# Forward column products as pairs of 64-row matmuls, one load queue at the head, a longer warm-up and a new order

## The chip, the core and the metric

The kernel runs on one core of one Trainium2 chip. The metric is the time of one execution in device microseconds; a figure for a kernel is the median of its runs. The core has a matrix engine (TensorE, PE in the profile), three engines for elementwise work (VectorE or DVE, ScalarE or ACT, GpSimd or POOL) and SyncE (SP), which here issues nearly all DMA transfers, one after the other, in one queue. Each engine works through its own list of instructions in order and waits on semaphores for the others.

## The reference

```python
x = A_x                                   # 1 x 2048 x 640, bf16
xn = _layernorm(x, axis=-1)               # rows of 640
X = rfft2(xn.astype(float32), axes=(-2, -1)) * (A_w_r + 1j * A_w_i)    # 2048 x 321
y = irfft2(X, s=(2048, 640)).astype(bfloat16)
h = (xn @ B_w_gate) * (xn @ B_w_up)       # 640 -> 1536
return x + y + h @ B_w_down               # 1536 -> 640
```

Two branches share the normalized rows: a filter in the two-dimensional frequency domain, and a gated product of matrices.

## The kernel before

**Tiling.** The 2048 rows are 16 blocks of 128. Partition p of block j holds row 16 p + j, so that a load of several blocks reads long pieces of memory. All matrix operands are bf16; PSUM has eight banks of 512 float32 values per partition.

**The work, by its names.** Every piece of work is a task with a name. Loads have names in ld_: ld_x (rows), ld_gw (gate and up weights; the first number is the first of 12 groups of 128 columns, the second is 0 for gate and 1 for up), ld_w (filter), ld_wd (down weights), ld_tf, ld_ti, ld_fd, ld_g, ld_sm1 (constant tables), ld_xr (rows again, for the final sum).

- Head. A warm-up task (L711 to L718) runs 40 matmuls of 128 columns on constants while the first rows load. Rows are normalized: for some blocks VectorE takes statistics (bn, ag), for others ScalarE does (sm at L738, sq at L747); ScalarE takes the root (sd, L772), VectorE the reciprocal (rs, L780) and the scaled rows (mul, L797). Blocks 0 to 3 are transposed by PE (T0, L816) and copied out of PSUM (eT0); blocks 4 to 15 by DMA transposes (xt, L804). After T0_0 a filler of six matmuls of 64 columns (L705) runs.
- Gated product. GU_f_b_w multiplies column group f, gate (w = 0) or up (w = 1), with the transposed rows from block b on: for single blocks and pairs of blocks two column groups at a time (L974, 128 or 256 columns), else 512 columns (L952). eG copies them to SBUF, H (L992, L994) multiplies gate by up.
- Forward transform. S1 to S5 on VectorE (L858 to L893) are the butterflies over the 640 columns, for groups of two or four blocks: S_0 blocks 0 and 1, S_1 blocks 2 and 3, S_2, S_3 and S_4 four blocks each. R_b (L906) is the column product of block b: five matmuls, each with 128 x 128 values of S's result as the stationary operand and a 128 x 128 table as the moving one. eR (through the copy helper L681 or L682) takes the 640 results per partition, a bank and a quarter of the next, to the buffer U. When all 16 R are done, D (L1035), C (L1054) and WM (L1071, L1074, with the filter) follow in eight rounds.
- Backward transform. SM, J, IA (L1117), I (L1145), then V1 to V5 on VectorE.
- Closing stage. ACC (L1222) is the down product, in three pieces of a chain of 12, which wait for ld_wd; IV (L1234) adds the inverse transform into the same bank; FINA and FIN add x, and st_out writes.

The table of R is half zeros: a block holds 64 x 2 rows that alternate along the partitions, and the transform is over 64, so for each parity the entries of the other are zero:

```python
fw = np.zeros((_R, _RR, 16, _G, 2, _RR), np.float64)      # _R = 64, _RR = 2
fw[:, r, tt, g, 0, r] = np.cos(ang)
```

**What sets the order.** The order of all tasks on all engines, and the PSUM bank of each, is written out by hand in the list _PLAN (L405): triples of task, engine and bank. replay (L151) assigns them; compute_waits (L196) makes the semaphore waits that the data and banks need. So each engine, and SP's queue, runs a fixed sequence, and a late task holds back all that stands behind it on its engine.

Around the change the sequences are: SP issues ld_x0a, ld_x1, ld_x2, ld_gw0_0, ld_x3, ld_gw2, ld_x4, ld_gw4, ld_x5, ld_sm1, ld_gw6_1, ld_gw8_1, ld_gw6_0, then xt7 (which waits for mul7), and then ld_gw8_0. ScalarE's queue issues ld_x0b and ld_gw0_1. VectorE runs both halves of bn1 between ag0 and rs_0. PE runs T0_1 after the filler, then GU_0_0; both GU_2_2 before R_0, R_1. The runs of R on PE, with GU between them, are R_0 R_1, R_2 R_3, R_6 R_4 R_7, R_5, R_10 R_11 R_8, R_9, R_12 R_13 R_15, R_14.

Of the kernel before, what the change touches and what calls it, by code (L numbers as in the profile page):

```python
# [241 lines left out]
_R = 64  # L242
_S1 = _S // _R
_RR = _S1 // 16
_G = 64 // _S1
# [10 lines left out]
def _build_tables():  # L256
# [6 lines left out]
    fw = np.zeros((_R, _RR, 16, _G, 2, _RR), np.float64)  # L263
    bw = np.zeros((16, _G, 2, _RR, _R, _RR), np.float64)
    for tt in range(16):
        for g in range(_G):
            q = tt * _G + g
            ang = two_pi * ((q * s2) % _R) / _R
            for r in range(_RR):
                fw[:, r, tt, g, 0, r] = np.cos(ang)  # L270
                bw[tt, g, 0, r, :, r] = np.cos(ang)
                if q:
                    fw[:, r, tt, g, 1, r] = -np.sin(ang)
                    bw[tt, g, 1, r, :, r] = np.sin(ang)
                else:
                    fw[:, r, tt, g, 1, r] = np.cos(math.pi * s2)
                    bw[tt, g, 1, r, :, r] = np.cos(math.pi * s2)
    sm[:, 1, :] = fw.reshape(128, 128)
# [122 lines left out]
def _d_act(n):  # L401
# [4 lines left out]
    (11, 4, -1), (10, 0, 5), (18, 2, -1), (12, 1, -1), (19, 2, -1), (20, 2, -1), (8, 3, -1), (0, 3, -1), (13, 4, -1),  # L406
    (28, 2, -1), (27, 2, -1), (14, 4, -1), (169, 4, -1), (15, 4, -1), (170, 1, -1), (21, 1, -1), (36, 1, -1), (22, 2, -1),
    (29, 2, -1), (30, 1, -1), (171, 4, -1), (172, 4, -1), (23, 2, -1), (24, 0, 0), (9, 0, 2), (37, 1, -1), (25, 1, -1),
    (38, 1, -1), (31, 2, -1), (32, 2, -1), (33, 0, 3), (26, 2, -1), (179, 0, 5), (39, 2, -1), (34, 2, -1), (40, 2, -1),
    (35, 2, -1), (43, 1, -1), (44, 1, -1), (45, 1, -1), (46, 2, -1), (47, 2, -1), (181, 0, 1), (182, 1, -1), (180, 1, -1),  # L410
    (183, 2, -1), (112, 2, -1), (41, 0, 7), (42, 1, -1), (189, 0, 6), (191, 0, 2), (184, 0, 0), (192, 1, -1), (190, 1, -1),
    (193, 2, -1), (48, 0, 4), (16, 4, -1), (186, 0, 1), (51, 2, -1), (50, 2, -1), (49, 1, -1), (185, 1, -1), (187, 1, -1),
    (188, 2, -1), (52, 2, -1), (54, 2, -1), (113, 2, -1), (53, 2, -1), (62, 1, -1), (63, 1, -1), (194, 0, 7), (64, 1, -1),
    (196, 0, 6), (174, 4, -1), (173, 4, -1), (55, 2, -1), (197, 1, -1), (195, 1, -1), (198, 2, -1), (114, 2, -1), (65, 1, -1),
    (204, 0, 0), (206, 0, 5), (56, 1, -1), (115, 2, -1), (57, 2, -1), (58, 2, -1), (116, 2, -1), (201, 0, 3), (205, 1, -1),
    (202, 1, -1), (66, 1, -1), (207, 1, -1), (199, 0, 2), (200, 1, -1), (208, 2, -1), (203, 2, -1), (67, 2, -1), (70, 2, -1),
    (211, 0, 1), (212, 1, -1), (17, 4, -1), (1, 4, -1), (72, 1, -1), (209, 0, 4), (117, 0, 0), (210, 1, -1), (118, 1, -1),
    (73, 1, -1), (74, 1, -1), (119, 0, 2), (121, 2, -1), (176, 4, -1), (221, 0, 7), (178, 4, -1), (175, 4, -1), (213, 2, -1),
    (216, 0, 5), (120, 1, -1), (217, 1, -1), (122, 2, -1), (68, 2, -1), (123, 2, -1), (75, 1, -1), (214, 0, 1), (215, 1, -1),
    (218, 2, -1), (124, 2, -1), (82, 1, -1), (76, 1, -1), (77, 2, -1), (125, 2, -1), (78, 2, -1), (71, 4, -1), (177, 4, -1),  # L420
    (59, 4, -1), (219, 0, 6), (60, 2, -1), (80, 2, -1), (226, 0, 4), (222, 1, -1), (220, 1, -1), (223, 2, -1), (224, 0, 0),
    (227, 1, -1), (225, 1, -1), (228, 2, -1), (130, 2, -1), (229, 0, 1), (230, 1, -1), (126, 0, 6), (127, 1, -1), (83, 1, -1),
    (128, 0, 2), (129, 1, -1), (231, 0, 0), (232, 1, -1), (233, 2, -1), (131, 2, -1), (236, 0, 4), (467, 4, -1), (237, 1, -1),
    (84, 1, -1), (85, 1, -1), (92, 1, -1), (234, 0, 5), (235, 1, -1), (238, 2, -1), (469, 4, -1), (69, 4, -1), (432, 4, -1),
    (3, 4, -1), (61, 4, -1), (86, 1, -1), (436, 4, -1), (87, 2, -1), (132, 2, -1), (241, 0, 7), (242, 1, -1), (93, 1, -1),
    (94, 1, -1), (246, 0, 2), (4, 4, -1), (431, 4, -1), (81, 4, -1), (239, 0, 3), (440, 4, -1), (240, 1, -1), (243, 2, -1),
    (244, 0, 4), (245, 1, -1), (247, 1, -1), (249, 0, 5), (251, 0, 0), (95, 1, -1), (96, 1, -1), (252, 1, -1), (250, 1, -1),
    (254, 0, 3), (255, 1, -1), (256, 0, 2), (257, 1, -1), (133, 2, -1), (248, 2, -1), (261, 0, 7), (134, 2, -1), (139, 0, 5),
    (135, 0, 0), (141, 0, 3), (97, 2, -1), (88, 2, -1), (90, 2, -1), (253, 2, -1), (266, 0, 2), (140, 1, -1), (262, 1, -1),
    (468, 4, -1), (437, 4, -1), (438, 4, -1), (472, 4, -1), (470, 4, -1), (100, 2, -1), (98, 2, -1), (258, 2, -1), (143, 2, -1),  # L430
    (142, 1, -1), (137, 0, 6), (138, 1, -1), (259, 0, 5), (260, 1, -1), (263, 2, -1), (144, 2, -1), (102, 1, -1), (267, 1, -1),
    (136, 1, -1), (264, 0, 6), (265, 1, -1), (268, 2, -1), (145, 2, -1), (269, 0, 5), (103, 1, -1), (270, 1, -1), (276, 0, 7),
    (277, 1, -1), (104, 1, -1), (271, 0, 1), (272, 1, -1), (273, 2, -1), (146, 2, -1), (274, 0, 0), (105, 1, -1), (275, 1, -1),
    (106, 1, -1), (147, 2, -1), (107, 2, -1), (281, 0, 3), (282, 1, -1), (279, 0, 7), (280, 1, -1), (284, 0, 0), (285, 1, -1),
    (286, 0, 2), (152, 0, 0), (153, 1, -1), (278, 2, -1), (473, 4, -1), (108, 2, -1), (435, 4, -1), (434, 4, -1), (466, 4, -1),
    (442, 4, -1), (439, 4, -1), (2, 4, -1), (91, 4, -1), (99, 4, -1), (154, 0, 6), (155, 1, -1), (89, 4, -1), (441, 4, -1),
    (79, 4, -1), (101, 4, -1), (110, 2, -1), (283, 2, -1), (156, 2, -1), (148, 0, 3), (149, 1, -1), (287, 1, -1), (289, 0, 5),
    (288, 2, -1), (157, 2, -1), (294, 0, 0), (295, 1, -1), (150, 0, 6), (291, 0, 1), (292, 1, -1), (290, 1, -1), (293, 2, -1),
    (296, 0, 4), (151, 1, -1), (297, 1, -1), (298, 2, -1), (301, 0, 0), (299, 0, 2), (309, 0, 1), (471, 4, -1), (109, 4, -1),
    (111, 4, -1), (433, 4, -1), (302, 1, -1), (300, 1, -1), (158, 2, -1), (7, 4, -1), (310, 1, -1), (311, 0, 3), (304, 0, 4),  # L440
# [81 lines left out]
def _build(nc, A_x, A_w_r, A_w_i, B_w_gate, B_w_up, B_w_down, out, opts=None):  # L522
# [3 lines left out]
    with es:  # L526
# [128 lines left out]
        b_sd = sch.buf("sd", 10 ** 9 + 30, 1)  # L655
        b_ve = sch.buf("ve", 10 ** 9 + 40, 1)

        xv = A_x[0].rearrange("(p j) d -> p j d", j=16)
        ov = out[0].rearrange("(p j) d -> p j d", j=16)
        wvs = [w_.rearrange("(k1 k2) l -> k1 k2 l", k2=_R) for w_ in (A_w_r, A_w_i)]  # L660
        gvs = [w_.rearrange("(j p) f -> p j f", p=128) for w_ in (B_w_gate, B_w_up)]
# [684 lines left out]
```

## Time and profile before

| what | value |
|---|---|
| median of three runs | 199.5 us (198.73 to 199.68) |
| profiled execution | 199.59 us |
| its span, first to last instruction | 197.9 us |
| mean granted TensorE clock | 0.991 |
| busy: PE, DVE, ACT | 192.2, 175.4, 137.9 us |
| DMA | 23.73 MB, mean 120 GB/s |

Some starts and ends, by the trace, in us: warm-up 0.85 to 5.06; T0_0 5.63; T0_1 7.44; first GU 7.88; mul0 5.18 to 5.57; mul3 ends 10.64; S5_0 ends 21.07; R_0 21.21; mul9 ends 30.0; xt5, the last of blocks 4 to 7, lands 36.8; first GU of blocks 4 to 7 38.2; S5_4 ends 69.35; R_12 69.61; first D 72.9; last IA 134.5; last matmul 195.4.

A line of the groups gives the source line, the engine, the operation, its tiles and shapes, the number of instructions, then busy us and mean ns of one, then the idle time before them and what ended it. A line of the timeline begins with start and duration. A line of the chain is a piece of the sequence of waits that ended last. Matmuls overlap: one lasts 219 ns at 128 columns, while the next starts 56 ns after it, so durations of PE are not its rate; starts are.

### The profile page before, as it was taken

To read this page: it belongs to the slowest core of one execution; us is meant where nothing else is said; L and a number is where in the kernel's file an instruction comes from. 1 tells how busy PE (TensorE), PEld (TensorE's weight loads), DVE (VectorE), ACT (ScalarE), POOL (GpSimd) and SP (SyncE) were. 2 spreads that over 40 slices of the span, in tenths; PEclk is the share of its full clock that TensorE was granted. 3 is DMA by queue.
4 is the path that set the end of the run, shared out by engine and by line. 5 is a ranking of instruction groups with operands and counts; after the bars stand their busy time and mean duration, and the time that the engine had idled before them with its cause. 6 is when DMAs were issued, how large, how long until landed. Compare 5 with 4: busy or idle time off the path is not lost.

```text
span 197.9 us, 4118 instructions
## 1 busy us (share of the span) xinstructions
PE 192.2 (97%) x1587; PEld 123.4 (62%) x1587; DVE 175.4 (89%) x364; ACT 137.9 (70%) x280; POOL 13.1 (7%) x22
## 2 busy tenths in 40 slices
PE   8699989999999999999999999999999999999995
PEld 8598735454454465556555555558677777777764
DVE  3588999999999989999999999985999999999843
ACT  3879998998976479998899998967504541440340
POOL 1000000000000000320330320330000000000000
PEclk9889999999999999999999999999999999999999
DMA  6999364979412016238492524004101252034242
GB/s 176 332 372 319 50 167 105 190 156 123 96 33 70 3 46 180 68 94 259 127 247 60 151 65 136 0 0 137 65 3 61 74 165 79 34 122 134 71 162 66
DMA packets 29666, 23.73 MB, mean 120 GB/s; under 512 B 10448, under 2 KB 27600, under 8 KB 29520
## 3 DMA queue, kind: packets, MB, share of 16 engines
q1 hardware_dynamic: 28848, 23.08, 43.8%
q10 hardware_dynamic: 800, 0.41, 0.7%
q8 instruction: 12, 0.20, 0.4%
q14 instruction: 6, 0.05, 0.1%
HBM read 18.89 MB, written 2.62 MB: 109 GB/s over the span
## 4 chain that ended last, share of the span: by engine, by line
PE 84%; DMA 7%; DVE 4%; ACT 3%; SPq 1%; issue 0%
PE ps L952 44%; PE ps L1222 25%; PE ps L1117 3%; PE ps L1035 2%; DMA arena<-in_B_w_gate_dram 2%; DMA arena<-in_B_w_down_dram 2%; PE ps L1054 2%; PE ps L1234 2%; PE ps L974 2%; DMA arena<-in_A_x_dram 2%; PE ps L906 2%; PE ps L1145 1%; ACT arena L738 1%; ACT arena L681 1%; DVE arena L797 1%; PE ps L816 1%
## 5 line engine op out<-in xcount | busy, mean ns | idle before, releaser
L681 ACT ACTIVATE arena<-ps 128x512 bf16<-128x512 f32 (+6 forms) x217 | 113.3, 579 | 50.8 <-PE ps L1234 18.0
L952 PE MATMUL ps<-arena 128*128 128x512 bf16 x420 | 97.4, 379 | 0.6 <-DMA arena<-in_B_w_gate_dram 0.6
L952 PEld LDWEIGHTS ps<-arena 128*128 128x128 bf16 x420 | 38.9, 98 | 42.1 <-DMA arena<-in_B_w_gate_dram 1.1
L1222 PE MATMUL ps<-arena 128*128 128x320 bf16 (+2 forms) x396 | 57.1, 295 | 0.2 <-DMA arena<-in_B_w_down_dram 0.2
L1222 PEld LDWEIGHTS ps<-arena 128*128 128x128 bf16 x396 | 37.4, 98 | 13.8 <-issue 0.5
L1071 DVE TENSOR_TENSOR arena<-ps,arena 128x256 bf16<-128x256 f32 x64 | 22.6, 415 | 1.9 <-PE ps L1054 1.8
L992 DVE TENSOR_TENSOR arena<-arena 128x512 bf16<-128x512 bf16 x42 | 17.9, 433 | 1.2 <-ACT arena L681 0.5
L974 PE MATMUL ps<-arena 128*128 128x128 bf16 (+1 forms) x160 | 15.3, 262 | 0.0
L974 PEld LDWEIGHTS ps<-arena 128*128 128x128 bf16 x160 | 13.7, 107 | 1.2
L682 POOL COPY arena<-arena 64x252 bf16<-64x252 bf16 x8 | 4.5, 568 | 100.7 <-DVE arena L1088 100.6
L1261 DVE TENSOR_TENSOR arena<-arena 128x640 bf16<-128x640 bf16 x15 | 7.1, 488 | 4.1 <-ACT arena L681 4.0
L747 ACT ACTIVATE arena<-arena 128x640 bf16<-128x640 bf16 x12 | 10.0, 836 | 0.1
L738 ACT ACTIVATE arena<-arena 128x640 bf16<-128x640 bf16 x12 | 8.9, 744 | 1.2 <-DMA arena<-in_A_x_dram 1.1
L1117 PEld LDWEIGHTS ps<-arena 128*128 128x128 bf16 x160 | 7.8, 116 | 2.5 <-ACT arena L681 0.2
L682 DVE CAST arena<-ps 128x320 bf16<-128x320 f32 (+3 forms) x11 | 7.0, 662 | 2.3 <-PE ps L1117 1.4
L1101 POOL TENSOR_SCALAR arena<-arena 64x252 bf16<-64x252 bf16 x8 | 7.9, 991 | 17.8 <-DVE arena L1088 17.4
L1117 PE MATMUL ps<-arena 128*128 128x64 bf16 x160 | 8.3, 198 | 0.0
L1035 PEld LDWEIGHTS ps<-arena 128*128 128x128 bf16 x160 | 6.5, 98 | 2.6 <-issue 0.3
L858 DVE TENSOR_TENSOR arena<-arena 128x768 f32<-128x768 bf16 (+1 forms) x10 | 7.9, 792 | 0.0
L1234 PE MATMUL ps<-arena 128*128 128x320 bf16 (+2 forms) x33 | 7.8, 295 | 0.0
L1035 PE MATMUL ps<-arena 128*128 128x64 bf16 (+1 forms) x160 | 7.0, 193 | 0.0
L1074 DVE TENSOR_TENSOR arena<-ps,arena 128x260 bf16<-128x260 f32 x16 | 7.0, 435 | 0.0
(61 smaller groups left out, 184.5 us busy)
## 6 DMA issues: line engine op xcount, KB each, us to landing
arena<-in_A_x_dram SPq DMA_DIRECT2D x19, 160.0 KB, 2.9
arena<-in_A_w_r_dram SPq DMA_DIRECT2D x30, 80.2 KB, 2.5
arena<-in_A_w_i_dram SPq DMA_DIRECT2D x30, 80.2 KB, 2.5
out_dram<-arena SPq DMA_DIRECT2D x15, 160.0 KB, 2.3
arena<-in_B_w_gate_dram SPq DMA_DIRECT2D x4, 320.0 KB, 6.3
arena<-in_A_x_dram SPq DMA_DIRECT2D x1, 1280.0 KB, 10.1
arena<-c_tf SPq DMA_DIRECT2D x4, 256.0 KB, 3.8
arena<-c_ti SPq DMA_DIRECT2D x2, 512.0 KB, 5.0
```

Source lines behind the costliest of these rows:

```text
L681: return c.e.activation(dst, src, _ACTF.Copy)
L682: return c.e.tensor_copy(dst, src)
L738: return c.e.activation(v_jk, v_x[:, b, :], _ACTF.Copy, scale=1.0 / _D, accum_out=v_m32[:, b:b + 1])
L747: return c.e.activation(v_jk, v_x[:, b, :], _ACTF.Square, scale=-1.0, bias=v_m32[:, b:b + 1], accum_out=v_ss[:, b:b + 1])
L952: ins = c.e.matmul(ps[:, bk, :], v_gw[:, w, j, ft, :], v_xt[:, j, rows], start=(j == 0), stop=(j == 4))
L974: ins = c.e.matmul(ps[:, bk, i * n:(i + 1) * n], v_gw[:, w, j, ft0 + i, :], v_xt[:, j, rows], start=(j == 0), stop=(j == 4))
L992: return c.e.tensor_tensor(v_ht[:, ft0, rows], gb[:, 0, :], gb[:, 1, :], _OP.mult)
L1035: ins = c.e.matmul(ps[:, bk + i, k * 64:k * 64 + n], v_uq[:, k, t + i, :], v_fd[:, k * 128 + w * n: k * 128 + w * n + n], start=True, stop ...
L1071: c.e.tensor_tensor(dst, xh, wv, _OP.mult)
L1117: ins = c.e.matmul(ps[:, bk, 64 * k:64 * k + 64], yl, v_ti[:, q, 0, :], start=True, stop=True)
L1222: ins = c.e.matmul(ps[:, bk, 0:sl3.stop - sl3.start], v_ht[:, ft, a * 128:(a + 1) * 128], v_wd[:, ft, sl3], start=(ft == _FT_ORDER[0]), st ...
L1234: return c.e.matmul(ps[:, bank_of(own), 0:sl3.stop - sl3.start], v_sm[:, 2, :], v_v[:, a, sl3], start=False, stop=True)
```

## The change

- R uses 64 rows at a time. Partitions now hold the two parities apart: partition r * 64 + s of block j holds row 32 s + 16 r + j (loads of x, the second loads of x, and the stores of the result are permuted so). The table of R becomes 128 x 64 without the zeros. Each of the five matmuls becomes two, one on partitions 0 to 63 into a bank and one on 64 to 127 into the next, each with 64 columns. eR reads the two banks interleaved, element by element. The table of IV is permuted to match.
- All gate and up loads go through SP; before, ld_gw0_1 was issued by ScalarE.
- The warm-up has 45 matmuls instead of 40, the filler five instead of six, and T0_1 comes after the filler by a dependence.
- The durations with which the planner reckons and _PLAN are new. SP: ld_x0a, ld_x2, ld_x1, ld_x3, ld_gw0_0, ld_gw0_1, ld_gw2, ld_x4, ld_gw4_1, ld_sm1, ld_gw4_0, ld_x5, ld_gw6, ld_gw8_1, ld_gw8_0, xt7, ld_w0_1_0, xt5, two filter loads, xt4, xt6; later ld_ti1 stands ahead of xt10, and ld_wd4 behind ld_wd6, ld_xr1 and ld_xr2. VectorE: rs_0 and mul0 before bn1, and both copies of T0_0 and eG_0_0 are its own; mul4 after S5_0; H_44 to H_47 spread over V1 to V5. PE: GU_0_0_0 before T0_1, one GU_2_2 after R_1 and R_0. The runs of R are now R_1 R_0, R_2 R_3, R_6 R_4, R_7 R_5, R_9 R_8, R_11, R_10, R_15 R_12 R_13, R_14. A few copies change between ScalarE and VectorE.

```diff
-    fw = np.zeros((_R, _RR, 16, _G, 2, _RR), np.float64)
-    bw = np.zeros((16, _G, 2, _RR, _R, _RR), np.float64)
+    fw = np.zeros((_RR, _R, 16, _G, 2), np.float64)
+    bw = np.zeros((16, _G, 2, _RR, _RR, _R), np.float64)
...
-                fw[:, r, tt, g, 0, r] = np.cos(ang)
-                bw[tt, g, 0, r, :, r] = np.cos(ang)
+                fw[r, :, tt, g, 0] = np.cos(ang)
+                bw[tt, g, 0, r, r, :] = np.cos(ang)
...
-    sm[:, 1, :] = fw.reshape(128, 128)
+    sm[:, 1, 0:64] = fw.reshape(128, 64)
...
 _PLAN = (
-    (11, 4, -1), (10, 0, 5), (18, 2, -1), (12, 1, -1), (19, 2, -1), (20, 2, -1), (8, 3, -1), (0, 3, -1), (13, 4, -1),
...
+        v_un = V("U").rearrange("p (n a c r) -> p n a c r", a=16, c=2, r=2)
...
-        xv = A_x[0].rearrange("(p j) d -> p j d", j=16)
-        ov = out[0].rearrange("(p j) d -> p j d", j=16)
+        xv = A_x[0].rearrange("(s r j) d -> r s j d", r=2, j=16)
+        ov = out[0].rearrange("(s r j) d -> r s j d", r=2, j=16)
...
-        nwarm = opts.get("nwarm", 10)
+        nwarm = opts.get("nwarm", 45)
...
-            for i in range(4 * nwarm):
+            for i in range(nwarm):
...
-                if b == 0:
-                    for f in fills:
-                        f.deps.add(t0)
+                if b < len(fills):
+                    fills[b].deps.add(t0)
+                if 0 < b <= len(fills):
+                    t0.deps.add(fills[b - 1])
...
-                        ins = c.e.matmul(psflat[:, bk * 512 + k * 128: bk * 512 + (k + 1) * 128], st, v_sm[:, 1, :],
-                                         start=True, stop=True)
+                        for r in range(2):
+                            ins = c.e.matmul(ps[:, bk + r, 64 * k:64 * k + 64],
+                                             st[64 * r:64 * r + 64], v_sm[64 * r:64 * r + 64, 1, 0:64],
+                                             start=True, stop=True)
...
-                    src = psflat[:, bk * 512: bk * 512 + 640].rearrange("p (j q m) -> p j q m", j=5, q=_NQ)
-                    return copy_on(c, v_u[:, :, :, b, :], src)
+                    src = ps[:, bk:bk + 2, 0:320].rearrange("p r (n c) -> p n c r", c=2)
+                    return copy_on(c, v_un[:, :, b], src)
...
-                    q="act" if w_ and i < 1 else "sp")
+                    q="sp")
```

## The prediction

> **What bounds the kernel now.** I read the page first, then the chain by time, the timeline of the first 20 us, and the groups by form.
>
> ```profile
> span 197.9 us, 4118 instructions
> PE 192.2 (97%) x1587; PEld 123.4 (62%) x1587; DVE 175.4 (89%) x364; ACT 137.9 (70%) x280; POOL 13.1 (7%) x22
> ```
>
> TensorE (PE) carries the chain (84% of it by the page), but its busy time says little, because matmuls overlap; starts say more. By the timeline PE starts the first real product (L974) at 7.88 us and the last matmul at about 195.4. From 12 us on its stream has few holes: 0.73 us before 29.00 and 0.37 before 139.87, both counted between starts, and 0.15 or less elsewhere. VectorE (DVE) idles, by its timeline, only some 2 us between 10.6 and 69 us: it is a second bound, close behind.
>
> ```profile
> 5.69 0.74 ACT L738 ACTIVATE arena<-arena 128x640 bf16<-128x640 bf16 x1 [1.11 <-DMA arena<-in_A_x_dram]
> ...
> 6.73 0.17 DVE L780 RECIPROCAL arena<-arena 128x1 f32<-128x1 f32 x1 [1.16 <-ACT arena L773]
> ...
> 7.44 0.45 PE L816 MATMUL ps<-arena 128*128 128x128 bf16 x5 [1.17 <-DVE arena L797]
> ...
> 7.88 2.13 PE L974 MATMUL ps<-arena 128*128 128x128 bf16 x20
> ```
>
> This is the head in the timeline: block 2 of x lands at 5.66, ScalarE (ACT) waits for it, VectorE waits for ACT, and PE for both. The 20 products at 7.88 take 2.13 us, 107 ns each, where later ones take 56. The stages tell why:
>
> ```profile
> 5.00:8.00 3.00, 1.26 (x20) 0.95 (x20) 1.46 (x8) 2.31 (x8) 0.00 (x0) 1.00 1.14 311
> 8.00:11.40 3.40, 3.40 (x35) 3.40 (x34) 2.24 (x8) 3.15 (x8) 0.00 (x0) 0.51 1.10 349
> 11.40:20.00 8.60, 8.60 (x108) 8.04 (x107) 7.42 (x23) 7.54 (x21) 0.00 (x0) 0.99 1.07 343
> ```
>
> (Length, then PE, weight loads, VectorE, ACT, GpSimd busy, clock, DMA.) After a stretch with PE busy 1.26 of 3.00 us, the granted clock is half for 3.4 us: 1.7 us of work lost.
>
> ```profile
> 23.91 0.29 SPq L804
> ...
> 24.26 4.70 DMA arena<-in_B_w_gate_dram
> ...
> 29.00 1.25 PE ps L952 x5
> ```
>
> In the chain, the last gate load stands on SP behind the transpose xt7, which waits for VectorE: hence PE's 0.73 us hole. Further on in the same chain ten matmuls of L906 (the column products R) take 0.56 us, 56 ns each.
>
> ```profile
> L1071 DVE TENSOR_TENSOR arena<-ps,arena 128x256 bf16<-128x256 f32 x64 | 22.6, 415 | 1.9 <-PE ps L1054 1.8
> L681 ACT ACTIVATE arena<-ps 64x642 bf16<-64x642 f32 x29 | 20.4, 704 | 1.6 <-PE ps L1035 1.0
> ...
> L681 ACT ACTIVATE arena<-ps 128x640 bf16<-128x640 f32 x15 | 10.3, 706 | 2.1 <-PE ps L906 2.0
> ...
> L906 PE MATMUL ps<-arena 128*128 128x128 bf16 x80 | 5.8, 219 | 0.0
> ```
>
> These groups price the new forms (second figure after the bar: mean ns).
>
> **The change, part by part.**
>
> *R as pairs.* Now 16 x 5 x 56 ns = 4.5 us. After: 16 x 10 matmuls of 64 rows and 64 columns. No row has 64-row products. Dearest row: the 128-row, 64-column products L1035 start 30 ns apart (x30 in 0.89 us of the chain): 0.30 us per block, +0.3 us in all. Cheapest: two halves run together, 5 x 30 = 0.15, -2.1 us. I take the middle, 0.23 (-0.8 us), no row being nearer. Going from 128 to 64 rows and back occurs 18 times in the new order (nine runs of R). Its price: nothing (128x512 and 128x64 products alternate without a hole) up to an emptied pipeline, 219 - 56 = 163 ns each, 2.9 us; a gain is excluded, since a switch saves no work. I take nothing, the nearest row, and keep 2.9 for the range. "TensorEngine Tiling (Array Packing)" of the Trainium skill (Key Properties) speaks against this: changing the tiling mode drains TensorE. No run here shows it; by that rule the 2.9 us would stand in the sum and the forecast would be near 200.8.
>
> *eR* reads the two banks alternately. Rows: 64x642 over two banks 704 ns, 128x640 706; strided L1071 on VectorE 415 for 256 elements, 1.62 ns each, against 435 for 260, 1.67 each, of the contiguous L1074. Price 0, and no row is quicker per element than 1.1 ns; ceiling: ACT's SBUF copies 64x1024 take 1.05 us, 1.03 ns per element, so 0.13 x 14 = 1.8 us on ACT, whose 30% idle time covers most.
>
> *x and out rows permuted.* Lengths stay. SP issues a plain load in 0.42 us, the two-part forms of the filter loads in up to 0.58: 0 to 0.16 each, on the last store too (0.2 at the end at most). Hidden in front: x1 then lands by 5.1, needed at 5.2.
>
> *Loads at the head.* gw0_1 leaves ACT's queue for SP; the order becomes x0a, x2, x1, x3, gw0_0, gw0_1. Landings before: x1 4.11, gw0_1 5.19, x2 5.66, gw0_0 6.76, x3 7.24: about 0.53 us per 160 KB. New: x2 4.1, x1 4.6, x3 5.2, gw0_0 6.2, gw0_1 7.3. The later weights keep their bytes ahead of them.
>
> *Head order.* VectorE now does rs_0 and mul0 ahead of bn1 (0.85 us): mul0 ends at 5.2 instead of 5.57. Warm-up: 45 instead of 40; the last nine at 56 ns, ends at 5.1-5.3, so T0_0 starts at 5.3, not 5.63. The filler has five matmuls instead of six: 0.03 us that nothing waits for. bn1 and ag1 end at 6.2, both copies of T0_0 (0.36 + 0.27) now on VectorE at 6.8: GU_0_0_0 starts at 6.9, 1.0 us earlier, but T0_1 (0.28) now comes after it. Between 5 and 8 us PE is then busy about 1.6 of 3.0 instead of 1.26; half clock after it is the nearer row, so I keep it. "TensorE: Matmul & The Clock Gate" of the skill (Part 1) makes activity over windows of about 3.4 us decide the clock; the 3.4 us at 0.51 agree, yet it gives no share from which a window counts as busy.
> VectorE: sm2 starts at 4.6 (x2), so sq3 ends at 8.8 and mul3 at 9.75 instead of 10.64: 0.9 us gained, though two copies (0.36, 0.38) moved in. mul4 and rs_4 (0.61) move behind S5_0, which ends at about 19.5 instead of 21.07. PE reaches R_1 after one GU_2_2 fewer (1.09): before 21.21 - 1.09 = 20.1, now 19.5 at half clock. Gain 0.6 for both.
>
> *Queue of SP.* gw8_0 moves ahead of xt7: the 0.73 us hole goes. Late next: xt5, xt4, xt6 now follow ld_w0_1_0, which waits for mul9 (about 29): three at 1.2 us and four filter loads at 0.45 to 0.6 put xt6's landing at 36.0 to 36.5; GU_0_4 is reached at 38.2 - 0.6 - 0.73 = 36.9. ld_ti1 (waits for mul15, about 56) now stands ahead of xt10, landing about 63, needed at 64. wd4 goes behind wd6, xr1, xr2, but 6.5 us of PE work lie between IA_31 and its first use and it lands after about 5: the 0.37 us hole at 139.87 goes. sm1 earlier: hidden. ld_w6_1_2 waits for WM_1 (79.4) ahead of five w4 loads, which then land by 85; WM_5 needs them at 89. ld_wd2 waits for IA_17 (116) ahead of w14_1_1, needed by WM_15 at 125. No cost by these.
>
> *Rest of the order.* PE's sets of work before R_14, C_0 and ACC_14 are the same as before. VectorE up to S5_4 does 0.74 more (the two copies). Later it gets eR_12 (0.82), JB_11 (0.45), eIA_22 (0.48), eG_46_1 and eG_49_0 (0.69 each), and gives ACT eG_27_0, eG_48_1 (0.69 each), eIA_4, eIA_21 (0.48 each), JA_11, JA_15 (0.42 each): 0.0 in all. GpSimd's JC and JD change places within pairs whose end stays. H_44 to H_47 come earlier among V1 to V5: 1.3 us sooner, with 1.0 us of VectorE's wait before V1_0 as cover; without that cover IV_4_0, which started 0.27 after V5_4, would wait up to 0.6.
>
> **The sum.** PE up to the last R could gain 0.6 + 0.73 + 0.8 = 2.1, but R_12 started 0.26 us after VectorE's S5_4, so VectorE limits it: 0.9 from mul3, plus half of the 1.75 us that it waited for ACT and PE between 12 and 69 us (0.27, 0.34, 0.46, 0.10, 0.48, 0.10), since the rows don't tell which of these waits end sooner (all or none of it goes into the range): 1.7, with little left for R's saving. Behind it -0.37 for wd, +0.4 given back in the closing stage by the H's. Total -1.7. The profiled execution took 199.59 (span 197.9 plus 1.7 around it), 0.1 above the median 199.5: 199.6 - 1.7 = 197.9 us.
>
> **Rivals.**
> 1. *The switches drain.* 18 x 0.163 + 0.3 = +3.2 in place of -0.8, against 0.6 + 0.73 + 0.37 gained; PE is then the later one and the H's cost nothing: +1.5, 201.1. For: R is scattered in nine runs on a gapless engine. Against: no hole at any change of shape so far. It ends slower from 0.385 us per R block, switches included (0.279 + 1.7 / 16).
> 2. *New waits eat the gain.* Margins of 0.2 to 0.7 us everywhere, a static order: one more 0.4 us stall in each of four stages (xt6, xt10, R_6 on S5_2, IV_4_0) leaves 199.3.
> 3. *The clock stays full.* 1.7 us of half clock go, PE is at R_1 at 18.1 and waits there for S5_0 at 18.8 (H_0, H_2 earlier): 0.7 more than planned, and VectorE, 0.7 earlier, lets 0.6 of R through: 196.6. For: busier before 8 us; against: 1.6 of 3.0 is nearer 1.26.
> 4. *The pairs do not run together*, 0.30 per block, no drain: PE's gain up to R_14 falls to 1.0, 0.7 below VectorE's limit: 198.6.
>
> **How the numbers follow.** Forecast 0.40 (197.2 to 198.6), rival 1 0.15, rival 2 0.21, rival 3 0.17, rival 4 0.07. About 0.5%, 1.0 us, is what a measurement of this kernel can tell from none (its three runs span 0.95). Below 198.5: 0.36 of the forecast, 0.17, 0.04: 0.57. Above 200.5: 0.13 of rival 1, 0.05 of rival 2: 0.18. The rest 0.25. The range 196.4 to 200.7 leaves out half of rival 1, and the far ends of rivals 2 and 3.
>
> **What would show it.** L906: starts of a pair 40 to 50 ns apart and no hole at either end (right), or holes near 160 ns (rival 1). First L974 near 6.9; the clock in 8 to 11.4 near 0.5. No wait of L952 for in_B_w_gate_dram, no wait for in_B_w_down_dram. eR near 706 ns. VectorE's S5_4 (L892) ending near 67.7, and R_12 right behind it. A PE hole anywhere over 0.7 us, or eR over 0.85 us, would make the prediction wrong.

## The result, and the profile after

The changed kernel takes 311.9 us (median of four runs, 311.2 to 312.5) where the kernel before takes 199.5: a ratio of 1.564, 95% interval 1.559 to 1.570. A time here is the median of all executions of a kernel, while a ratio, with its 95% interval in brackets, leaves out those over 1.5% above the fastest of the same kernel (one of e1_split, two of e3_pairs). The prediction said 197.9 us, range 196.4 to 200.7. It was wrong by 114 us, and no rival came near.

The page of the changed kernel (the PE, DMA and GB/s rows are 40 slices of the span; the last line is the shares of the chain of waits):

```profile
span 309.7 us, 4277 instructions
PE 211.4 (68%) x1671; PEld 128.4 (41%) x1671; DVE 176.1 (57%) x365; ACT 138.2 (45%) x279; POOL 13.0 (4%) x22
...
PE   5165390059999999999999966963970693915620
...
DMA  0352212354642951446341031010111111111111
GB/s 28 123 159 94 86 56 91 107 138 102 129 101 37 230 158 37 128 105 158 94 107 47 1 96 47 5 39 27 39 48 48 37 41 49 51 39 48 48 45 39
...
DMA 40%; PE 40%; SPq 11%; DVE 3%; ACT 2%; issue 1%; DVEq 0%
```

The work is nearly what it was: VectorE busy 176.1 us against 175.4, ScalarE 138.2 against 137.9. TensorE, 97% busy before, is at 68%. The chain, 84% TensorE before, is now half DMA and its issue on SP. The TensorE row shows where: the first nine slices (70 us) and the last seventeen. From the 29th slice on (217 us) the DMA row reads 1 and the GB/s row 37 to 51: the transfers are late, and yet most of the DMA engines do nothing.

The chain of the changed kernel by time (start, duration, what), its long pieces:

```profile
27.48 35.63 DMA arena<-in_A_x_dram
...
65.19 6.55 PE ps L954 x20
...
201.78 11.96 DMA out_dram<-arena
...
218.52 13.81 DMA arena<-in_A_x_dram
...
234.06 11.65 DMA arena<-in_A_x_dram
...
248.46 10.86 DMA out_dram<-arena
...
260.74 11.85 DMA out_dram<-arena
```

The load of blocks 8 to 15 is in flight for 35.6 us (10.1 before, both from the start of its issue). In the closing stage the second loads of x and the stores hold the chain for 11 to 14 us at a time. All are transfers whose rows the change permutes. How many DMA engines they use is read from a stretch in which nothing else moves, the first window here. The windows of the changed kernel (length, busy time of PE, weight loads, VectorE, ACT, GpSimd, then granted clock, DMA share, GB/s):

```profile
50.00:58.00 8.00, 0.00 (x0) 0.00 (x0) 0.00 (x0) 0.00 (x0) 0.00 (x0) 0.50 0.13 54
50.00:60.00 10.00, 0.00 (x0) 0.00 (x0) 0.00 (x0) 0.00 (x0) 0.00 (x0) 0.50 0.17 55
...
220.00:240.00 20.00, 9.99 (x79) 6.87 (x76) 10.14 (x15) 2.83 (x6) 0.00 (x0) 0.92 0.13 48
...
260.00:280.00 20.00, 9.58 (x52) 5.95 (x52) 9.04 (x20) 2.14 (x6) 0.00 (x0) 0.68 0.13 46
```

and of the kernel before, while it loaded the same rows, with weights beside them:

```profile
10.00:20.00 10.00, 10.00 (x122) 9.44 (x120) 8.69 (x26) 8.80 (x24) 0.00 (x0) 0.93 1.07 339
```

A share of 0.13 of sixteen engines is two engines. In 50 to 58 us everything waits for the one load, at 54 GB/s; up to 60 us the share is 0.17, since weights set in behind it. The kernel before moved 339 GB/s. SP pays too; its queue in the changed kernel:

```profile
0.81 6.61 SPq L676 DMA_DIRECT2D arena<-in_A_x_dram  x4
7.46 3.20 SPq L676 DMA_DIRECT2D arena<-in_B_w_gate_dram  x1
...
34.74 12.56 SPq L676 DMA_DIRECT2D arena<-in_B_w_gate_dram  x1
```

and in the kernel before:

```profile
0.81 1.34 SPq L675 DMA_DIRECT2D arena<-in_A_x_dram  x3
2.20 0.43 SPq L675 DMA_DIRECT2D arena<-in_B_w_gate_dram  x1
2.67 0.52 SPq L675 DMA_DIRECT2D arena<-in_A_x_dram  x1
```

The same four issues took 1.9 us in all in the kernel before; here they take 6.6. The plain weight loads behind them are slow to issue as well (3.2 us, later 12.6, against 0.43 to 2.42 before), so permuted transfers hold up what stands behind them in the queue. How they do it, no run shows.

Where the 111.8 us of the two spans lie, from the starts of three kinds of instruction in the traces (all in us; the experiments of the next section are in the same table, and "end" is the end of the span):

| kernel | first product | first D | first D to last IA | last IA to last matmul | last matmul to end | span |
|---|---|---|---|---|---|---|
| before | 7.9 | 72.9 | 61.7 | 60.7 | 2.5 | 197.9 |
| after | 18.4 | 115.2 | 61.8 | 119.7 | 13.0 | 309.7 |
| e2_rows | 17.7 | 116.1 | 61.7 | 114.3 | 7.2 | 299.3 |
| e8_r4 | 12.6 | 95.4 | 61.7 | 80.7 | 4.6 | 242.4 |
| e8_r16 | 8.9 | 75.3 | 61.7 | 60.8 | 2.9 | 200.7 |
| e1_split | 9.9 | 77.3 | 61.7 | 65.4 | 7.2 | 211.6 |
| e9_halves | 9.5 | 76.4 | 61.7 | 64.5 | 7.2 | 209.8 |
| e13_evenodd | 9.9 | 75.1 | 61.7 | 64.4 | 7.0 | 208.3 |
| e10_cols | 8.0 | 72.0 | 61.7 | 61.9 | 3.9 | 199.6 |
| e12_stores | 7.7 | 70.6 | 61.7 | 90.0 | 9.6 | 231.9 |
| e4_order | 7.1 | 70.5 | 61.8 | 61.1 | 2.5 | 195.8 |
| e11_warm40 | 6.8 | 70.2 | 61.8 | 61.1 | 2.5 | 195.5 |
| e7_pairs | 7.5 | 70.1 | 61.8 | 61.1 | 2.5 | 195.4 |

After against before: +42.3 us before the first D, nothing in the middle, +58.9 in the closing stage, +10.5 behind the last matmul. The middle loads the filter and reads no x: it takes the same time in every run.

### The profile page after: what moved, and what is told of

Read it like the earlier page. It is cut to its first block, busy times and chain, and to the rows that moved or that the text cites. A ratio compares the mean times of both kernels' runs of the same rounds, so it can differ in the third digit from the quotient of the medians.

```text
span 309.7 us, 4277 instructions
## 1 busy us (share of the span) xinstructions
PE 211.4 (68%) x1671; PEld 128.4 (41%) x1671; DVE 176.1 (57%) x365; ACT 138.2 (45%) x279; POOL 13.0 (4%) x22
## 3 DMA queue, kind: packets, MB, share of 16 engines
HBM read 18.89 MB, written 2.62 MB: 69 GB/s over the span
## 4 chain that ended last, share of the span: by engine, by line
DMA 40%; PE 40%; SPq 11%; DVE 3%; ACT 2%; issue 1%; DVEq 0%
PE ps L954 30%; DMA arena<-in_A_x_dram 20%; DMA out_dram<-arena 17%; SPq L676 11%; PE ps L1224 4%; DMA arena<-in_B_w_down_dram 3%; PE ps L1119 2%; ACT arena L682 2%; DVE arena L1263 2%; PE ps L1037 2%; PE ps L1056 2%; PE ps L907 1%; DVE arena L1180 0%; ACT arena L737 0%; DVE arena L1245 0%
## 5 line engine op out<-in xcount | busy, mean ns | idle before, releaser
L954 PE MATMUL ps<-arena 128*128 128x512 bf16 x420 | 98.7, 385 | 18.8 <-ACT arena L682 18.8
L1224 PE MATMUL ps<-arena 128*128 128x320 bf16 (+2 forms) x396 | 70.1, 337 | 42.5 <-ACT arena L682 32.3
L1224 PEld LDWEIGHTS ps<-arena 128*128 128x128 bf16 x396 | 42.3, 111 | 64.2 <-ACT arena L682 33.9
L976 PE MATMUL ps<-arena 128*128 128x128 bf16 (+1 forms) x160 | 17.9, 282 | 16.8 <-DVE arena L880 8.7
L976 PEld LDWEIGHTS ps<-arena 128*128 128x128 bf16 x160 | 14.6, 114 | 19.5 <-DMA arena<-in_B_w_gate_dram 17.3
L996 DVE TENSOR_TENSOR arena<-arena 128x256 bf16<-128x256 bf16 (+1 forms) x8 | 2.8, 350 | 22.2 <-ACT arena L682 22.2
L755 DVE BATCH_NORM_STATS2 arena<-arena 128x6 f32<-128x320 bf16 x8 | 3.6, 485 | 20.6 <-DMA arena<-in_A_x_dram 20.6
L683 DVE CAST arena<-ps 128x512 bf16<-128x512 f32 (+4 forms) x12 | 7.8, 673 | 2.4 <-PE ps L954 0.9
L1236 PE MATMUL ps<-arena 128*128 128x320 bf16 (+2 forms) x33 | 8.4, 298 | 0.0
L1147 PE MATMUL ps<-arena 128*128 128x128 bf16 x80 | 6.7, 225 | 2.3 <-ACT arena L682 2.3
```

The lines of the kernel that those rows point to most:

```text
L683: return c.e.tensor_copy(dst, src)
L954: ins = c.e.matmul(ps[:, bk, :], v_gw[:, w, j, ft, :], v_xt[:, j, rows], start=(j == 0), stop=(j == 4))
L976: ins = c.e.matmul(ps[:, bk, i * n:(i + 1) * n], v_gw[:, w, j, ft0 + i, :], v_xt[:, j, rows], start=(j == 0), stop=(j == 4))
L1224: ins = c.e.matmul(ps[:, bk, 0:sl3.stop - sl3.start], v_ht[:, ft, a * 128:(a + 1) * 128], v_wd[:, ft, sl3], start=(ft == _FT_ORDER[0]), st ...
```

## The experiments

The theory, called A in the expectations: a transfer is spread over as many DMA engines as the outermost dimension of its pattern in memory has entries, up to 16. The permuted rows are walked as two parities by 64 rows, so two engines work. The rivals: the pairs or the new order cost the time, or the loss comes from rows that no longer lie in rising order, or each such transfer is slow in itself whatever else is in flight.

### One part of the change at a time

**e2_rows**: the kernel before, with the rows permuted and nothing else.

```diff
-        xv = A_x[0].rearrange("(p j) d -> p j d", j=16)
-        ov = out[0].rearrange("(p j) d -> p j d", j=16)
+        xv = A_x[0].rearrange("(s r j) d -> r s j d", r=2, j=16)
+        ov = out[0].rearrange("(s r j) d -> r s j d", r=2, j=16)
...
-                fw[:, r, tt, g, 0, r] = np.cos(ang)
+                fw[r, :, tt, g, 0, r] = np.cos(ang)
```

> The kernel before with the row permutation alone: loads, stores and both tables permuted, R still five matmuls of 128 rows, old order, old queues, old warm-up. Theory A: nearly the whole loss, 290 to 320 us. Theory B: 199 to 201 us.

Measured: 301.1 us, ratio 1.510 (1.502 to 1.518). Its page:

```profile
span 299.3 us, 4118 instructions
...
PE 39%; DMA 36%; SPq 13%; DVE 8%; ACT 1%; issue 1%; DVEq 0%
```

The permutation alone makes 101.7 of the 112 us, in the same two places of the table.

**e1_split**: the changed kernel, each transfer of x, each second load and each store issued as two, one for each parity (64 partitions).

```diff
+            parts = [(dst[64 * r:64 * r + 64], src[r]) for r in range(2)] if two else [(dst, src)]
...
-                return c.e.dma_start(dst, src)
+                return [c.e.dma_start(d_, s_) for d_, s_ in parts]
...
+                return [c.e.dma_start(dst[r], src[64 * r:64 * r + 64]) for r in range(2)]
```

(The last line is that of the stores.)

> The changed kernel with one thing undone in form: each load and store of permuted rows (ld_x, ld_xr, st_out) is issued as two transfers of 64 partitions, one for each parity, instead of one whose source begins with a dimension of 2. Same bytes, same order, same tables, same pairs. Theory A (a transfer whose slowest dimension is 2 is moved by 2 of the 16 DMA engines: in the changed kernel's stretch 50 to 60 us, with only x under way, the DMA share is 0.17, and in the closing stage 0.10 to 0.13): the transfers are quick again and the time falls from 312 to 197 to 200 us, SP paying some 40 more issues of 0.4 us. Theory B (the new order or the one queue starves the head and the end, and the slow transfers are only crowded): above 280 us, as the order is untouched.

Measured: 213.0 us, ratio 1.069 (1.064 to 1.073). The same rows go to the same places, and 99 of the 112 us are gone: it was the shape of the transfer, not where the rows lie. But 13.5 us stay, which I had not expected; e9, e10 and e13 below are for that.

**e3_pairs**: the kernel before, its order and queues, with the pairs and the split transfers.

```diff
-                        ins = c.e.matmul(psflat[:, bk * 512 + k * 128: bk * 512 + (k + 1) * 128], st, v_sm[:, 1, :],
-                                         start=True, stop=True)
+                        for r in range(2):
+                            ins = c.e.matmul(ps[:, bk + r, 64 * k:64 * k + 64],
+                                             st[64 * r:64 * r + 64], v_sm[64 * r:64 * r + 64, 1, 0:64],
+                                             start=True, stop=True)
...
+            parts = [(dst[64 * r:64 * r + 64], src[r]) for r in range(2)] if two else [(dst, src)]
...
+                return [c.e.dma_start(dst[r], src[64 * r:64 * r + 64]) for r in range(2)]
```

> The kernel before with R as pairs of 64 rows and the permuted rows moved by two transfers of 64 partitions each; old order, old warm-up, old queues. In the changed kernel's trace a pair of halves starts 3 to 4 ns apart, pairs 29 ns apart, and each change between 128 and 64 rows costs 96 ns (312 instead of 216, 122 instead of 26). So R costs 16 x 0.147 + 16 x 0.096 (eight runs) = 3.9 us instead of 4.5: PE 0.6 us better, hidden where VectorE is late, and about 40 more issues on SP. Theory A: 198.5 to 200.5. If pairs are what costs (theory C): above 203.

Measured: 211.8 us, ratio 1.057 (1.052 to 1.063). It says nothing of the pairs, since the split transfers cost as much here as in e1_split.

**e4_order**: the changed kernel with plain rows and the 128-row R: the order, the queue of the loads and the warm-up alone.

```diff
-        xv = A_x[0].rearrange("(s r j) d -> r s j d", r=2, j=16)
-        ov = out[0].rearrange("(s r j) d -> r s j d", r=2, j=16)
+        xv = A_x[0].rearrange("(p j) d -> p j d", j=16)
+        ov = out[0].rearrange("(p j) d -> p j d", j=16)
...
-                        for r in range(2):
-                            ins = c.e.matmul(ps[:, bk + r, 64 * k:64 * k + 64],
-                                             st[64 * r:64 * r + 64], v_sm[64 * r:64 * r + 64, 1, 0:64],
-                                             start=True, stop=True)
+                        ins = c.e.matmul(psflat[:, bk * 512 + k * 128: bk * 512 + (k + 1) * 128], st, v_sm[:, 1, :],
+                                         start=True, stop=True)
```

> The changed kernel without pairs and without the row permutation: R as five matmuls of 128 rows, plain rows, but the new order, one load queue at the head and the longer warm-up. Theory A: 197 to 199.5 us, as the prediction reckoned the order (hole before the last gate load and hole before the down weights gone, head about 1 us earlier), with R at 0.28 per block. Theory B: above 280 us.

Measured: 197.8 us, ratio 0.992 (0.989 to 0.995). It is 1.6 us faster than the kernel before. Half of that or more goes with the granted clock of TensorE, which differs between executions of one and the same kernel. Of 48 executions of the kernel before, measured beside the experiments, 31 have a mean clock of 0.991, as in its profile (half clock from 8 to 11.4 us), and take 198.8 to 200.3 us, median 199.6; 17 have 0.999 or 1.000 and take 197.5 to 198.7, median 198.1. All seven of e4_order have 1.000. Beside the three full-clock executions of its own round (median 198.6) the order gains 0.8 us; e11_warm40 below, the same order, gains 0.2 (197.7 against 198.0, nine executions each). So at the same clock the order is worth 0.2 to 0.8 us, and the rest goes with the full clock, which its executions have more often.

**e7_pairs**: the changed kernel with plain rows, pairs kept.

```diff
-        xv = A_x[0].rearrange("(s r j) d -> r s j d", r=2, j=16)
-        ov = out[0].rearrange("(s r j) d -> r s j d", r=2, j=16)
+        xv = A_x[0].rearrange("(p j) d -> p j d", j=16)
+        ov = out[0].rearrange("(p j) d -> p j d", j=16)
```

> The kernel after with the plain rows of before in all transfers of x and of the result, and nothing else taken back: R runs as pairs of 64-row matmuls, eR reads two banks. Since the rows are then not split by parity, the column transform mixes other rows than the reference's; the amount of work is the same. It is the price of the pairs alone, against the order alone (197.8 us, ratio 0.992 to before). By the trace of after (two halves start 3 to 4 ns apart, the next pair 29 to 30 ns later, so 0.147 us per block instead of 0.279; 96 ns at each of 18 changes between 128 and 64 rows) TensorE gains 0.4 us, of which VectorE's limit lets through part: 197.2 to 197.9 us, ratio 0.989 to 0.993. If the pairs cost more than they save (my rival of drained switches, 2.9 us), 199 us or more.

Measured: 197.4 us, ratio 0.992 (0.989 to 0.995), inside the range that was expected. The chain by time shows the products R of the last four blocks, in e4_order

```profile
67.41 0.84 PE ps L906 x15
68.25 1.08 PE ps L952 x5
69.33 0.28 PE ps L906 x5
69.60 1.08 PE ps L952 x5
```

and in e7_pairs

```profile
67.07 0.54 PE ps L907 x30
...
68.80 0.25 PE ps L907 x10
69.05 1.19 PE ps L954 x5
```

Three blocks in a row take 0.54 us instead of 0.84. A single one takes 0.25 instead of 0.28, and the five 128-row products behind it 1.19 instead of 1.08. By the starts of single matmuls in the changed kernel's trace, the two halves of a pair begin 3 or 4 ns apart and the next pair 26 later, so a block costs 5 x 29.5 = 147 ns instead of 279. From the last 512-column product to R it takes 312 ns instead of 216, from R's last matmul to the next product 122 where the step within R is 26: 96 ns for a change from 128 rows to 64, and 96 for the way back. In sum 16 x 0.132 saved less 18 x 0.096 spent is 0.4 us; the first D of e7_pairs comes 0.45 us before that of e4_order. The times cannot tell the two kernels apart.

### What in the permutation costs the time

**e8_r4 and e8_r16**: e2_rows with other outermost dimensions, 4 by 32 and 16 by 8.

```diff
-        xv = A_x[0].rearrange("(s r j) d -> r s j d", r=2, j=16)
-        ov = out[0].rearrange("(s r j) d -> r s j d", r=2, j=16)
+        xv = A_x[0].rearrange("(s r j) d -> r s j d", r=4, j=16)
+        ov = out[0].rearrange("(s r j) d -> r s j d", r=4, j=16)
```

(r=16 in the second one.)

> The kernel before, with the rows of the x loads, of the second x loads and of the stores permuted with an outermost dimension of 4 (32 rows inside) instead of the 2 by 64 of the change; everything else, R's 128-row table too, is as before, so the column transform mixes other rows than the reference's. Theory A (a transfer is spread over as many DMA engines as its outermost dimension has entries): 4 of 16 engines work in the x loads, with a DMA share near 0.25 while x5 alone moves (it was 0.17 with 2 by 64), and the time lies about half way down from the 301 us of 2 by 64: 225 to 255 us. Theory B (the loss comes from rows that are no longer in rising order in memory along the partitions, whatever the outermost count): again 290 to 305 us.

> As the run with an outermost dimension of 4, but 16 by 8: the rows are permuted as thoroughly, and each piece of memory is as long as in the other permutations. Theory A: all 16 engines work, the time is that of the kernel before, 198.5 to 201 us. Theory B: 290 to 305 us.

Measured: 244.4 us (ratio 1.228, 1.218 to 1.238) and 203.5 us (1.022, 1.012 to 1.032). Outermost counts of 2, 4, 16 and 128 (the kernel before) give 301, 244, 203 and 199 us. Theory A had named the place of the first, and the rival, 290 to 305 for both, falls. The number of engines can be read too. The windows of e8_r4, while the load of blocks 8 to 15 moves alone, and in the closing stage:

```profile
34.00:39.00 5.00, 0.00 (x0) 0.00 (x0) 0.00 (x0) 0.00 (x0) 0.00 (x0) 0.50 0.25 102
...
180.00:200.00 20.00, 14.92 (x96) 10.07 (x97) 14.83 (x20) 5.00 (x12) 0.00 (x0) 0.83 0.23 73
```

A share of 0.25 is four engines, at 102 GB/s where two moved 54. But e8_r16 is 2.5 us above its range. With 16 by 8 the engines are all busy and still move less. The windows of e8_r16:

```profile
10.00:20.00 10.00, 10.00 (x120) 9.58 (x119) 7.45 (x22) 8.30 (x23) 0.00 (x0) 1.00 1.09 235
```

The kernel before moves 339 GB/s in that stretch at a share of 1.07. An issue on SP takes 0.60 us (median) in place of 0.43. Why the engines are slower in this pattern stays open.

**e12_stores**: e4_order with only the stores permuted 2 by 64.

```diff
-        ov = out[0].rearrange("(p j) d -> p j d", j=16)
+        ov = out[0].rearrange("(s r j) d -> r s j d", r=2, j=16)
```

> The order alone (197.8 us), with the stores of the result permuted 2 by 64 in single transfers and all loads plain, so that the rows of the result lie elsewhere than the reference's. In the closing stage of the kernel after, loads and stores together (5.24 MB) ran at 41 to 49 GB/s with a DMA share of 0.12 to 0.13, and the stage took 119.7 us instead of 60.7: 5.24 MB at 45 GB/s are 116 us. If the rate of two engines is what costs (theory A), the stores alone need 2.62 MB / 45 GB/s = 58 us, which the 61 us of the stage nearly cover: 199 to 206 us, a DMA share near 0.13 in the last 60 us. If every permuted transfer costs about its 10 to 12 us of the chain whatever else is in flight (rival), 16 stores through two buffers need 80 to 96 us: 220 to 235 us.

Measured: 233.6 us, ratio 1.175 (1.168 to 1.182): the rival's number, not mine. ScalarE in the timeline (idle time before it in brackets), where it fills the two rows of the output buffer:

```profile
155.63 0.44 ACT L682 ACTIVATE arena<-ps 128x320 bf16<-128x320 f32 x1 [4.07 <-DMA out_dram<-arena]
159.34 1.69 ACT L682 ACTIVATE arena<-ps 128x320 bf16<-128x320 f32 x4 [3.27 <-DMA out_dram<-arena]
...
167.23 1.03 ACT L682 ACTIVATE arena<-ps 128x320 bf16<-128x320 f32 x2 [3.05 <-DMA out_dram<-arena]
170.63 1.10 ACT L682 ACTIVATE arena<-ps 128x320 bf16<-128x320 f32 x3 [2.36 <-DMA out_dram<-arena]
```

Two stores go out together (150.6 is the issue of the second), the first has landed at 155.6, the second 3.7 us later; in the next round the distance is 3.4. 160 KB in 3.7 us are 44 GB/s, so the rate of two engines is as theory A had it, and the rival's fixed 10 to 12 us for every transfer is not what happens, although its number came out: the second of two takes only 3.7 us more. What failed is the cover. I had laid 58 us of storing beside 61 us of work, but the buffer has two rows, so ScalarE, VectorE and SP refill it only after a landing, and for 2 to 3 us of each round (159.3 to 161.5, 170.6 to 173.0) no store is under way. A round of two blocks takes 11.2 us in the mean (chain pieces of stores begin at 150.60, 162.01, 173.57 and, six rounds after the first, at 218.11), eight rounds 90 us: the stage took 90.0. In the changed kernel the second loads of x share the two engines (0.13 from 220 to 240 us, with both under way), so a round has four transfers: an estimate of 8 x 4 x 3.7 = 118 us against 119.7 measured.

### What remains with split transfers

**e9_halves**: e4_order with each transfer of x and of the result issued as two of 64 partitions, rows plain.

```diff
-                return c.e.dma_start(dst, src)
+                return [c.e.dma_start(dst[64 * r:64 * r + 64], src[64 * r:64 * r + 64]) for r in range(2)]
```

> The order, queue and warm-up of the change with plain rows and the 128-row R (197.8 us in its own run), but each transfer of x, each second load of x and each store is issued as two transfers of 64 partitions. It prices what kept the version with split permuted transfers at 213 us. If the splitting itself is the cause (60 more issues on SP at about 0.42 us, or 64 partitions being slower to fill than 128), it takes 208 to 214 us. If the cause was the order in memory of the permuted rows or the pairs, it takes 197.5 to 200 us.

**e10_cols**: the same number of issues, but each with 128 partitions and half of the columns or blocks.

```diff
-                return [c.e.dma_start(dst[64 * r:64 * r + 64], src[64 * r:64 * r + 64]) for r in range(2)]
+                k_ = dst.shape[1] // 2
+                return [c.e.dma_start(dst[:, k_ * r:k_ * r + k_], src[:, k_ * r:k_ * r + k_]) for r in range(2)]
```

> As the run with halves of 64 partitions, but the two transfers keep all 128 partitions and share the columns (single blocks: 320 columns each; x4 and x5: half of the blocks each). The number of issues is the same. If the issues alone cost the time, it equals the run with halves of 64 partitions within 2 us; if 64-partition transfers are slow in themselves, it takes 198 to 203 us, with the head's 60 to 70% of the DMA rate back (330 GB/s and more in 10 to 30 us instead of 258).

**e13_evenodd**: as e9_halves, but the two take the even and the odd partitions.

```diff
-                return [c.e.dma_start(dst[64 * r:64 * r + 64], src[64 * r:64 * r + 64]) for r in range(2)]
+                return [c.e.dma_start(dst[r:128:2], src[r:128:2]) for r in range(2)]
```

> As the run with halves of 64 partitions (212.5 us), but the two transfers take the even and the odd partitions, so that each of them reaches over all 128 partitions with 64 of them; the number of issues and the bytes per piece are as there. If a transfer is slow because it has 64 partitions, again 210 to 214 us and about 260 GB/s in 10 to 30 us. If it is slow because its partitions lie in one half of the memory (fewer ports), it equals the run with halves of the columns, 200.5 to 203 us, with 340 GB/s and more in 10 to 20 us.

Measured, in the order of the three: 212.5 us (ratio 1.067, 1.061 to 1.073), 201.7 (1.014, 1.008 to 1.020) and 209.9 (1.053, 1.047 to 1.058). So the splitting into 64 partitions explains what e1_split kept, with plain rows and without pairs: 14.8 us over e4_order, of which the 41 more issues alone, at the full width, cost 3.9. e13_evenodd has the rate of the one theory and nearly the time of the other. The windows of e9_halves, then those of e13_evenodd:

```profile
10.00:20.00 10.00, 9.60 (x113) 9.12 (x112) 8.01 (x23) 6.07 (x17) 0.00 (x0) 0.77 1.13 256
...
10.00:20.00 10.00, 10.00 (x117) 9.76 (x118) 7.51 (x22) 5.73 (x16) 0.00 (x0) 0.74 1.08 351
```

351 GB/s against 256: halves that lie in one end of the partitions are slower to fill, halves spread over all are not. "SBUF — State Buffer" of the Trainium skill (Door 1: The DMA port swizzle) makes the rate depend on the number of ports that the partitions reach, which the two rates agree with. But in time this is worth 2.7 us only. For the other 8.2 us over e10_cols the issue is the likely cause. The chain by time, e10_cols

```profile
2.66 0.43 SPq L684
...
3.14 0.43 SPq L684
```

and e13_evenodd

```profile
2.97 0.60 SPq L679
...
3.61 0.60 SPq L679
```

An issue of 64 partitions takes SP 0.60 us, one of 128 takes 0.43. The eight issues of the head end at 4.5 us in e10_cols, at 6.1 in e13_evenodd, and at 2.6 for four whole ones in e4_order; the first weights stand behind them. TensorE then has little to do before 8 us (1.05 of 3 us in e13_evenodd) and runs at a clock of 0.54 from 8 to 11.4, where e10_cols has 1.00. At the other end the stores are late by the same issues: 7.0 us between the last matmul and the end, against 3.9 and 2.5. An estimate for the issue alone is 41 x 0.17 = 7 us; the late weights and the clock come with it. I did not measure these shares apart from one another, nor did I try the second halves on another engine's queue, so this split is argued and not shown.

### The warm-up

**e11_warm40**: e4_order with the 40 warm-up matmuls of before.

```diff
-        nwarm = opts.get("nwarm", 45)
+        nwarm = opts.get("nwarm", 40)
```

> The order alone (197.8 us, granted clock 1.0 between 8 and 11.4 us, where before had 0.51), with 40 warm-up matmuls instead of 45. If the longer warm-up keeps the clock up, the clock between 8 and 11.4 us is near 0.5 again and the time 198.2 to 199.4 us. If the products that come earlier and closer together do it, the clock stays at 1.0 and the time at 197.5 to 198.1 us.

Measured: 197.8 us, ratio 0.996 (0.992 to 0.999), its median equal to that of e4_order. The longer warm-up does not change the median. Three of the 12 executions have a mean clock of 0.991, against none of the seven of e4_order and one of the 11 of e7_pairs; that is too few to say whether the longer warm-up makes the half clock rarer. The windows of e11_warm40

```profile
5.00:8.00 3.00, 2.28 (x33) 1.84 (x31) 2.75 (x11) 2.94 (x9) 0.00 (x0) 1.00 1.09 313
8.00:11.40 3.40, 3.38 (x61) 3.22 (x59) 3.31 (x12) 2.85 (x8) 0.00 (x0) 1.00 1.10 349
```

show the clock full where the kernel before had 0.51. But it isn't the busy share of that window either: e7_pairs keeps the full clock after 1.42 of 3 us, e13_evenodd and the kernel before lose it after 1.05 and 1.26, and e8_r16 keeps it after 0.72. Each of these is one profiled execution, and the kernel before has the half clock in two executions of three. What decides is open.

## Why the prediction was wrong, step by step

***x and out rows permuted*: this step failed, and it is the whole error** (without the permutation, in e7_pairs, the changed kernel takes 197.4 us). It said "Lengths stay", priced the new pattern at 0 to 0.16 us for each issue, and called it hidden. I costed the issue and the bytes and not the engines that share them. Measured: two engines, 44 to 55 GB/s instead of 340, issues of a permuted load of up to 4.1 us, 42 us lost in front and 69 us behind. "DMA: Bandwidth & Descriptors" of the Trainium skill (Why a DMA increments its semaphore by 16 and not by 1, and Rules for kernel authors) says that the largest number up to 16 that divides the outermost dimension of both patterns is the number of engines. I did not set that sentence beside the diff, where the 2 stands written in the rearrangement; the runs with 2, 4 and 16 agree with it. With that count the trace of before gives the price, as an estimate: with 16 engines, 340 GB/s are 21 for each, so two engines are 43, and 2 x 2.62 MB at that rate are 122 us in a stage of 61 (119.7 measured).

**The rivals** held none of this. All four moved a term of one or two microseconds, and the one that was to end slower was put on TensorE. A rival for each new access pattern was missing.

***Loads at the head***, without the permutation (e4_order): x2, x1, x3, gw0_0 and gw0_1 landed at 3.6, 4.8, 5.7, 6.9 and 8.2 us, foretold 4.1, 4.6, 5.2, 6.2 and 7.3. The order was right; the weights took 1.2 to 1.3 us each where I had 1.0 to 1.1.

***Head order***: first product 7.07 (said 6.9), mul3's end 9.54 (9.75), right. TensorE was busy 2.42 of the 3 us before 8 us, not 1.6, and half clock "as the nearer row" was wrong: it stayed full in all seven executions, as in rival 3. The row of before could not decide it alone, since the same kernel also runs at the full clock. S5_0 ended at 17.55, not 19.5, and R_1 began at 18.53.

***Queue of SP***: both holes of TensorE are gone, as said. The groups of e4_order (last figure: idle time before) have none for the products that had them:

```profile
L952 PE MATMUL ps<-arena 128*128 128x512 bf16 x420 | 96.6, 379 | 0.0
...
L1222 PE MATMUL ps<-arena 128*128 128x320 bf16 (+2 forms) x396 | 57.0, 295 | 0.0
```

***The sum***: VectorE does limit the stage up to the last R, but its last S5 ended at 66.81 us and not 67.7, since its idle time from 10.6 us up to there fell from 2.1 us to 1.0. The first D comes 2.4 us earlier (said 1.7), the closing stage is 0.3 longer (said 0.0): -2.0 by the spans in place of -1.7. The median of the order alone is 197.8 where I forecast 197.9 for the whole, and that is luck: the forecast kept the half clock on both sides, while the gain at the same clock is 0.2 to 0.8 us. Two slips in the arithmetic matter little: 0.9 and half of 1.75 are 1.8 and not 1.7, and four stalls of 0.4 us give rival 2 199.5 and not 199.3. Rival 3, the full clock at 196.6, had the clock right and the time 1.2 too low, since VectorE sets the end of that stage.

***R as pairs***: "0.23 us per block", no charge for the changes. Measured 0.147 for a block and 0.096 for a change of rows: 0.255 a block with the changes, -0.4 us in place of -0.8. Charging nothing for the change of rows was the wrong end of the range. The rule of "TensorEngine Tiling (Array Packing)" of the Trainium skill (Key Properties) that I set against it is right in its sign, and the price here is 0.096 us and not the 0.163 of an emptied pipeline. Rival 1, slower from 0.385 us a block, fails by its size, and rival 4, pairs that do not run together, falls: the halves begin 3 or 4 ns apart.

***eR***: 708 ns against 706, price 0 as said. (The ceiling of 0.13 us does not follow from its row: 640 elements at 1.03 ns are 0.66 us, less than the 0.706 of before. Nothing rests on it.) By form, in the changed kernel:

```profile
L682 ACT ACTIVATE arena<-ps 128x640 bf16<-128x640 f32 x14 | 9.8, 708 | 1.5 <-PE ps L907 1.5
```

The test that I gave myself, "a PE hole anywhere over 0.7 us", named the right sign: the timeline of the changed kernel has one of 18.8 us ahead of the first 512-column product, where ScalarE waits for the last load of x.

## What to carry to other kernels

Before a layout is changed for a compute engine's sake, write down the outermost count of every access pattern that it touches on both sides, and price each transfer by that count, by its partitions, and by its issue: here a saving of 0.4 us on TensorE was bought with 2 of 16 DMA engines on a third of the bytes. A transfer that is "beside other work" is hidden only as far as its buffers reach: with two rows of output the producer waits for each landing. And where several edits come together, measure them one at a time: the order was worth 1.6 us by the medians, 0.2 to 0.8 at the same granted clock, the warm-up nothing that could be measured, and both were buried. A gain of that size has to be read together with the clock of each execution, which here goes with 1.5 us.

## What the runs showed of the hardware that I had not expected

- Rate against the outermost count of the pattern, rows otherwise permuted alike: 2 gives 44 to 55 GB/s at a DMA share of 0.13, 4 gives 102 at 0.25, 16 by 8 gives 235 with all engines busy, plain 128 gives 340 (the last two with weights beside the rows).
- Behind permuted transfers the issue of a plain weight load took up to 12.6 us (2.4 at most in the kernel before); SP is then held for the others too.
- SP needs 0.60 us to issue a transfer of 64 partitions and 0.43 for 128; two halves of 64 cost nearly three times one whole.
- With halves of 64 partitions the head (10 to 20 us) moved 256 GB/s when they are the lower and the upper 64, 351 when they are the even and the odd.
- Two 64-row matmuls on different halves and banks start 3 or 4 ns apart; going from 128 rows to 64 or back costs 96 ns.
- One kernel, run again, has a mean granted TensorE clock of 0.999 or 1.000 in some executions (17 of 48, median 198.1 us) and of 0.991 in the others (31 of 48, median 199.6), which in the one that was profiled is half clock for 3.4 us.
